# Sixteen on-chip copies of rounded q and k: issued from ScalarE's DMA queue instead of SyncE's

## The chip, the cores and the metric

The kernel runs on one core of one Trainium2 chip. The metric is device time in microseconds of one execution, as the median of several runs. The core has five engines that run side by side, each with its own in-order instruction queue: TensorE (PE, matrix products and transposes; its weight loads are shown apart as PEld), VectorE (DVE), ScalarE (ACT), GpSimd (POOL) and SyncE (SP, which computes nothing and here issues nearly all transfers). A transfer (DMA) is issued by an instruction on some engine's queue, and is then carried out by 16 DMA engines that belong to none of them. An instruction waits on semaphores until what it needs is done; while it waits, what stands behind it on its queue waits too.

## The reference, cut to what matters

Three blocks in a row, all in float32:

```python
# q, k, v: (2, 8, 768, 64); proj: (64, 6)
q_bits = einsum('bhsd,dk->bhsk', q, proj) > 0        # six sign bits for each row
k_bits = einsum('bhsd,dk->bhsk', k, proj) > 0
mask = bucket(q_bits)[..., :, None] == bucket(k_bits)[..., None, :]
scores = where(mask, q @ k.T / sqrt(64), -1e9)
attn = exp(scores - max(scores)); attn /= sum(attn) + 1e-9
x = (attn @ v) laid out as (2, 768, 512)

u = x + real(fft(fft(x, axis=1), axis=2))            # second block
un = layernorm(u)
y = u + relu(un @ w_ch1) @ w_ch2                     # 512 -> 2048 -> 512

theta = y @ w_theta                                  # third block
t = w_tok_r @ (y * cos(theta)) + w_tok_i @ (y * sin(theta))
out = (y + t) + relu((y + t) @ w_ch)
```

## The kernel before, in words

Precision is kept by splitting: an operand is stored as a rounded part and the remainder, and a product is taken as three (or fewer) products of the parts. Weights arrive as 64-bit floats and are turned into such pairs on the chip: a load into a tile `r` (`from_f64`, lines 169 to 181), two ScalarE activations and a VectorE operation on it, then a rounded copy by ScalarE (`w1h`, `w2h`) and a remainder by GpSimd (`w1l`, `w2l`). Every such load is issued on SyncE's queue, and reuses a tile that the GpSimd subtraction before has to be done with.

**The stages.** Attention of batch 0 runs first, two heads at a time (`attention_first`). Then come, interleaved, attention of batch 1 (`attention`, line 416), Fourier transform, layer norm and multilayer perceptron of batch 0, and the conversion of `w1` and `w2`. After that the same for batch 1, then the third block for both batches. In the trace attention of batch 1 prepares its first head at about 134 us and ends near 360 us; the multilayer perceptron of batch 0 begins inside it.

**Attention of batch 1.** `prep(b, j)` (lines 271 to 319) prepares a pair of heads: it loads q, k (tile `tt`) and v (`vr`), scales k, forms the sign bits with four matmuls per half, and then for each of the two heads fills a stack `s` (tag `stk`, two buffers) of four rows of [128, 768]: planes 0 and 1 are the left operand of the scores, planes 2 and 3 the right one. Since a head has only 64 dimensions, one half of the 128 partitions (`dd`) holds the rounded q or k, and the other half (`oo`) holds the remainder or a one-hot image of the bucket, which adds the mask to the scores in the same matmuls. Eight heads are prepared in this way, so each instruction of the loop over `h` (line 297) occurs eight times in the profile, once for q and once for k:

- ScalarE writes the rounded q (plane 0, line 302) and the rounded k (plane 2, line 305): `stk<-tt`.
- A DMA copies each of them to a second place in the same stack (lines 303 and 306): `stk<-stk`, on SyncE's queue. These are the lines of the change.
- GpSimd writes the remainders (lines 304 and 307): `stk<-tt,stk`.
- TensorE spreads the bits (`pat`), and ScalarE turns them into the one-hot halves (line 315): `stk<-pss,hb`.

`attn_S` (line 339) then takes four matmuls per block of 128 rows of q: `pss<-stk`. They need all planes. VectorE finds the maximum (`nm<-pss`), ScalarE takes the exponential (`p<-pss,nm`), ScalarE or GpSimd makes the rounded 16-bit part and GpSimd the remainder (`p<-p`, `pt<-p,pt`), a transposing DMA on SyncE's queue turns the block (`pt<-p`, `pt<-pt`, `x<-p`, by which buffer it uses), and TensorE multiplies with v (`pso<-vv,...`, `attn_AV`).

**What sets the order.** In this stage no order is written out by hand. Each piece of work gets a due time (`at(...)`, with a start, a pace per block, and a lead for `prep`), and a planner, which simulates the engines while the program is built, puts the instructions of each engine in one fixed order from the due times and from what it reckons to be ready. On the chip each queue keeps that order. The wrapper classes `AC`, `SY`, `PL`, `V`, `PE` (line 73) stand for the five queues.

Of the kernel before, what the change touches and what calls it, by code (L numbers as in the profile page):

```python
# [33 lines left out]
def f(t):  # L34
    return t.bitcast(F32)
# [35 lines left out]
def fused_kernel(ctx, tc, A, out):  # L71
    nc = tc.nc
    V, AC, PE, PL, SY = (Ordered(tc, e) for e in (nc.vector, nc.scalar, nc.tensor, nc.gpsimd, nc.sync))
# [4 lines left out]
    def mk(p, shape, dt, tag, **kw):  # L78
        return p.tile(shape, dt, tag=tag, name=tag, **kw)

    def mm(o, l, r, st, sp):
        PE.matmul(o, l, r, start=st, stop=sp)

    def pl_copy(out, in_, scale=1.0):
        PL.tensor_scalar(out=out, in0=in_, scalar1=scale, scalar2=0.0, op0=ALU.mult, op1=ALU.add)

    def stt(eng, out, in0, in1, op, scale=1.0):
        if eng is V:
            return V.scalar_tensor_tensor(out=out, in0=in0, scalar=scale, in1=in1, op0=ALU.mult, op1=op)
        assert scale == 1.0  # L90
        return eng.tensor_tensor(out=out, in0=in0, in1=in1, op=op)
# [23 lines left out]
    def PS(k):  # L115
        n = turn[k] % sum(c for _, c in ring[k])
        turn[k] += 1
        for p, c in ring[k]:
            if n < c:
                w = [128, 2, 512] if k == "s" else [128, 512]  # L120
                tag = "psm" if p in [x[0] for x in ring["m"]] else "ps" + k
                live[k] = p.tile(w, F32, tag=tag, name=tag)
                return live[k]
            n -= c
# [27 lines left out]
    def fill(n, k="o"):  # L152

        for _ in range(n):
            PE.matmul(live[k][:, 392:512], pat[:, 0], pat[:, 1, 0:120], start=True, stop=True)
# [115 lines left out]
    def prep(b, j):  # L271

        tt = mk(at_p, [128, 2, S], F32, "tt")
        ld = {"s": SY, "a": AC, "p": PL}[T["ld"][b]]
        vr = mk(at_p, [128, 2 * NT * (D + 1)], F32, "vr")
        for o, i in ((tt[:, 0], A["qT"]), (tt[:, 1], A["kT"]), (vr, A["v"])):
            ld.dma_start(out=o, in_=i[b, j])
        pl_copy(tt[:, 1], tt[:, 1], 0.125)
        v2 = mk(vv_p, [128, 2, 2 * NT * (D + 1)], F16, "vv")

        def values():
            AC.activation(out=v2[:, 0], in_=vr, func=AF.Copy, scale=VS)
            stt(V, v2[:, 1], vr, v2[:, 0], ALU.subtract, VS)

        if j:
            values()
        yield
        st = []
        bits = mk(at_p, [64, 2, 384], BF16, "bits")
        ps = PS("s")  # L290
        into = [ps[:, g, 0:384] for g in range(2)]
        for g in range(2):
            for qk in range(2):
                mm(into[g][32 * qk:32 * qk + 32], projb, tt[:, qk, 384 * g:384 * g + 384], True, True)
        V.tensor_scalar(out=bits, in0=ps[0:64, :, 0:384], scalar1=0.0, scalar2=None, op0=ALU.is_gt)
        made[4 * b + j] = [st, v2.rearrange("p a (h k c) -> p a h k c", h=2, k=NT)]
        for h in range(2):
            yield
            dd, oo = half[h], half[1 - h]
            s = mk(st_p, [128, 4, S], F32R, "stk")  # L300
            st.append(s)
            AC.activation(out=s[dd, 0], in_=tt[dd, 0], func=AF.Copy)
            SY.dma_start(out=f(s[dd, 1]), in_=f(s[dd, 0]))
            stt(PL, s[oo, 1], tt[dd, 0], f(s[dd, 0]), ALU.subtract)
            AC.activation(out=s[dd, 2], in_=tt[dd, 1], func=AF.Copy)
            SY.dma_start(out=f(s[oo, 3]), in_=f(s[dd, 2]))
            stt(PL, s[dd, 3], tt[dd, 1], f(s[dd, 2]), ALU.subtract)
            pp = PS("s")
            for g in range(2):
                mm(pp[:, g, 0:384], pat[0:64, h], bits[:, g], True, True)  # L310
            if b and not j and not h:
                fill(T["i0"])
            for qk in range(2):
                i = half[h if qk else 1 - h]
                AC.activation(out=s[oo, 2 * qk].rearrange("p (a n) -> p a n", a=2), in_=pp[i, :, 0:384],
                              func=AF.Sign if qk else AF.Relu, bias=hb[i, qk:qk + 1])
            if not j and not h:
                values()
        yield
# [96 lines left out]
    def attention(b, t0, pace, lead, hi_eng, lo_eng, after=lambda b, j: None):  # L416
        x_t[b] = mk(x_p, [128, NT, DM], F32, "x")
        n, w = 0, soft["p2"][0].shape[1]
        for j in range(4):
            i = 4 * b + j  # L420
            if i not in made:
                at(t0 + pace * n - lead)
                with after_gate("p1" if b else None):
                    run(prep(b, j))
            st, vv = made[i]
            for hh in range(2):
                h = PO[j] + 4 * hh
                at(t0 + pace * n)
                o = PS("o")[:, 0:NT * (D + 1)].rearrange("p (t d) -> p t d", t=NT)
                for t in range(NT):  # L430
                    at(t0 + pace * n)
                    ps = attn_S(st[hh], t)
                    fill(T["i1"][n] if n < len(T["i1"]) else 0)
                    with after_gate(0 if b and n >= T["n1"] else "ln0" if b and n >= T["n0"] else None):
                        p, m = attn_exp(ps)
                    if not t % w:
                        p2 = soft_tile("p2")
                    with after_gate(0 if b and n >= T["n1"] else None):
                        attn_split(p, p2[:, t % w].bitcast(F16).rearrange("p (a n) -> p a n", a=2), hi_eng(n), lo_eng(n))
                    if t % w == w - 1:  # L440
                        pt, trans = transposed(p2)
                        for i in range(w):
                            attn_AV(o, pt[:, 12 * i:12 * i + 12], vv, hh, t - w + 1 + i)
                    n += 1
                    if j < 3 and [hh, t] in T["ps"]:
                        at(t0 + pace * n - lead)
                        if [hh, t] == T["ps"][0]:
                            new = prep(b, j + 1)
                        next(new)
                at(t0 + pace * n - 30)  # L450
                attn_norm(b, h, o)
# [733 lines left out]
```

## Time and profile before

| | us |
|---|---|
| runs shown (3) | 729.13, 730.92, 737.44 |
| median | 730.92 |
| the profiled execution, whole | 728.28 |
| its span, first to last instruction | 726.5 |
| PE / PEld busy in the span | 664.8 / 510.9 |
| DVE / ACT / POOL busy in the span | 402.6 / 372.7 / 370.1 |

All times of rows are microseconds from the start of the profiled span, durations in a summary of a tile are nanoseconds. Line 62 is the helper through which almost every operation is issued, so the rows are told apart by their tiles: `stk<-tt` writes `stk` from `tt`. "SPq" is SyncE's queue. A row of the timeline gives the start, the time to the end of the last of its instructions, engine, line, operation, tiles, the count, and in brackets the idle time of the engine just before and what ended it. A row of a table of stretches gives the stretch, its length, then for PE, PEld, DVE, ACT and POOL the busy time with the number of instructions, then TensorE's granted clock (1.00 is its full speed), the share of the 16 DMA engines that was busy, and the rate of transfers. In a table of waits a row reads: who waited, for whom, total, number of times, longest.

### The profile page before, as it was taken

How to read it: one execution, taken by the hardware profiler on the slowest of the kernel's cores; microseconds unless marked ns; L12 is line 12 of the kernel's file. 1: busy time of each engine (PE TensorE's matmuls, PEld its weight loads, DVE VectorE, ACT ScalarE, POOL GpSimd, SP SyncE). 2: the span in 40 equal slices, each digit the busy share in tenths (PEclk: the TensorE clock that was granted, in tenths of full speed). 3: DMA queues.
4: the chain of work that ended last, by engine and by line, in shares of the span. 5: the costliest groups of instructions: out<-in, count | busy, mean ns of one | idle time of the engine just before them, and what ended most of it. 6: DMA issues, size and time to landing. Idle time of an engine off the chain costs nothing.

```text
span 726.5 us, 13450 instructions
## 1 busy us (share of the span) xinstructions
PE 664.8 (92%) x5424; PEld 510.9 (70%) x5424; DVE 402.6 (55%) x655; ACT 372.7 (51%) x597; POOL 370.1 (51%) x312
## 2 busy tenths in 40 slices
PE   5798988669668898999999999999999899999998
PEld 2365556557557655786686786687485599999997
DVE  1566787865999665543377583255422476751222
ACT  2565565766988898773423152065325676730010
POOL 3787789586878888776660020033403446930000
PEclk9999999978699999999999999999999999999999
DMA  9896967459889999776560043011004631720202
GB/s 327 186 187 141 157 121 142 93 164 213 197 206 240 269 231 253 151 145 124 102 195 27 13 120 65 1 45 30 1 1 145 223 89 39 234 81 25 88 1 87
DMA packets 161469, 93.68 MB, mean 129 GB/s; under 512 B 137088, under 2 KB 147584, under 8 KB 161408
## 3 DMA queue, kind: packets, MB, share of 16 engines
q1 hardware_dynamic: 159472, 86.27, 51.3%
q0 software_dynamic: 1936, 6.57, 2.6%
q8 instruction: 42, 0.69, 0.4%
q14 instruction: 19, 0.16, 0.1%
HBM read 49.82 MB, written 6.29 MB: 77 GB/s over the span
## 4 chain that ended last, share of the span: by engine, by line
PE 48%; POOL 10%; issue 9%; DMA 6%; ACT 5%; DVE 4%; POOLq 0%; SPq 0%; DVEq 0%; ACTq 0%
PE psm L62 31%; PE psf L62 14%; POOL p L62 3%; ACT r L62 2%; PE pso L62 2%; POOL w1l L62 2%; DMA x<-p 2%; POOL stk L62 2%; PE pss L62 1%; DMA r<-in_wtok 1%; DMA r<-in_w 1%; POOL pt L62 1%; DVE r L62 1%; ACT stk L62 1%; POOL w2l L62 1%
## 5 line engine op out<-in xcount | busy, mean ns | idle before, releaser
L62 PE MATMUL psm<-unT,w1h 128*128 128x256 f16 x768 | 130.4, 274 | 0.1
L62 PE MATMUL psm<-unT,w1l 128*128 128x256 f16 x384 | 105.2, 274 | 0.0
L62 DVE SCALAR_TENSOR_TENSOR r<-r 128x512 uint32<-128x512 uint32 (+1 forms) x64 | 64.6, 1016 | 51.9 <-ACT r L62 49.2
L62 PEld LDWEIGHTS <-w1h 128*128 128x128 f16 (+1 forms) x774 | 75.1, 99 | 15.5 <-issue 4.5
L62 PEld LDWEIGHTS <-hh 128*128 128x128 f16 x384 | 37.1, 98 | 42.8 <-issue 2.2
L62 POOL TENSOR_TENSOR w1l<-r,w1h 128x384 fp32r<-128x384 f32 (+1 forms) x36 | 41.9, 1178 | 43.5 <-ACT w1h L62 43.5
L62 PE MATMUL pss<-stk 128*128 128x384 f32 x192 | 48.8, 384 | 15.2 <-ACT p L62 9.4
L64 PE MATMUL pss<-stk 64*128 64x384 f32 (+1 forms) x288 | 55.4, 470 | 6.4 <-ACT p L64 3.2
L62 DVE TENSOR_REDUCE nm<-pss 128x1 f32<-128x768 f32 x48 | 44.9, 949 | 29.0 <-PE pss L62 28.8
L62 PE MATMUL psm<-w2h,hl 128*128 128x512 f16 x192 | 60.3, 379 | 0.0
L62 PE MATMUL psm<-w2l,hh 128*128 128x512 f16 x192 | 59.8, 379 | 0.2 <-POOL w2l L62 0.2
L62 ACT ACTIVATE r<-r,chalf 128x512 uint32<-128x512 uint32 (+1 forms) x64 | 46.1, 720 | 26.2 <-DMA r<-in_wtok 10.2
L62 PE MATMUL psm<-w2h,hh 128*128 128x512 f16 x192 | 59.3, 379 | 0.0
L62 POOL TENSOR_TENSOR p<-p,p 128x768 f16<-128x768 f32 x32 | 54.7, 1715 | 6.6 <-ACT p L62 5.5
L62 ACT ACTIVATE p<-pss,nm 128x768 f32<-128x768 f32 x48 | 42.5, 892 | 28.1 <-DVE nm L62 23.3
L62 DVE SCALAR_TENSOR_TENSOR hl<-psm,hh 128x512 f16<-128x512 f32 x48 | 32.8, 687 | 41.9 <-ACT hh L62 41.8
L64 DVE TENSOR_REDUCE nm<-pss 128x1 f32<-128x768 f32 x48 | 43.6, 950 | 19.9 <-PE pss L64 19.8
L62 ACT ACTIVATE hh<-psm 128x512 f16<-128x512 f32 x48 | 28.2, 590 | 40.4 <-PE psm L62 40.4
L62 PEld LDWEIGHTS pss<-stk 128*128 128x128 f32 x192 | 34.6, 204 | 20.2 <-ACT p L62 11.9
L62 PEld LDWEIGHTS <-w1l 128*128 128x128 f16 x384 | 37.7, 98 | 5.7 <-issue 1.2
L62 ACT ACTIVATE r<-r 128x512 f32<-128x512 f32 (+1 forms) x64 | 39.5, 618 | 0.0
L62 POOL TENSOR_TENSOR stk<-tt,stk 64x768 fp32r<-64x768 f32 x16 | 31.1, 1945 | 11.5 <-issue 9.6
(322 smaller groups left out, 1552.2 us busy)
## 6 DMA issues: line engine op xcount, KB each, us to landing
r<-in_w SPq DMA_DIRECT2D x32, 512.0 KB, 4.5
r<-in_wtok SPq DMA_DIRECT2D x24, 384.0 KB, 3.8
vr<-in_v SPq DMA_DIRECT2D x8, 390.0 KB, 3.6
stk<-stk SPq DMA_DIRECT2D x16, 192.0 KB, 3.8
xT<-xs SPq DMA_DIRECT2D x12, 256.0 KB, 2.6
xt<-xT SPq DMA_DIRECT2D x4, 768.0 KB, 5.8
ct<-in_ct POOLq DMA_DIRECT2D x4, 579.0 KB, 7.3
sn<-in_sn POOLq DMA_DIRECT2D x4, 576.0 KB, 8.2
```

Source lines behind the costliest of these rows:

```text
L62: return fn(*a, **k)
L64: self.last = fn(*a, **k)
```

## The change

Lines 303 and 306: the copies are issued with `AC.dma_start` instead of `SY.dma_start`. What is copied, from where to where, is the same, and nothing else is edited. The planner orders the program anew when it is built.

```diff
             AC.activation(out=s[dd, 0], in_=tt[dd, 0], func=AF.Copy)
-            SY.dma_start(out=f(s[dd, 1]), in_=f(s[dd, 0]))
+            AC.dma_start(out=f(s[dd, 1]), in_=f(s[dd, 0]))
             stt(PL, s[oo, 1], tt[dd, 0], f(s[dd, 0]), ALU.subtract)
             AC.activation(out=s[dd, 2], in_=tt[dd, 1], func=AF.Copy)
-            SY.dma_start(out=f(s[oo, 3]), in_=f(s[dd, 2]))
+            AC.dma_start(out=f(s[oo, 3]), in_=f(s[dd, 2]))
             stt(PL, s[dd, 3], tt[dd, 1], f(s[dd, 2]), ALU.subtract)
```

## Rows read from the trace of the kernel before

**Rows 1.** The page: span, and busy time of each engine in it.
```profile
span 726.5 us, 13450 instructions
PE 664.8 (92%) x5424; PEld 510.9 (70%) x5424; DVE 402.6 (55%) x655; ACT 372.7 (51%) x597; POOL 370.1 (51%) x312
```

**Rows 2.** Table of stretches: attention of batch 1, and what follows it.
```profile
133.00:325.00 192.00, 161.38 (x1592) 125.43 (x1591) 136.22 (x209) 154.98 (x231) 155.51 (x108) 0.91 0.89 200
325.00:525.00 200.00, 199.77 (x1476) 140.81 (x1474) 100.99 (x197) 73.53 (x125) 62.47 (x63) 1.00 0.29 68
525.00:726.00 201.00, 195.72 (x1155) 177.72 (x1153) 82.19 (x122) 76.08 (x144) 57.21 (x52) 1.00 0.29 92
```

**Rows 3.** Tile stk, from 133 to 325 us: counts, min/median/max duration, landing time.
```profile
L62 ACT ACTIVATE stk<-tt x16: 822/827/841, 133.8 to 316.0; 64x768 fp32r<-64x768 f32 x16
L62 SPq DMA_DIRECT2D stk<-stk x16: 461/472/953, 134.6 to 318.3; - x16
DMA to landing us min/median/max: 2.6/3.8/6.0
```

**Rows 4.** Waits of SyncE's queue, 133 to 325 us.
```profile
SPq L62 <- POOL w1l L62: 33.0, 15, 6.7
SPq L62 <- ACT stk L62: 15.0, 12, 6.7
```

**Rows 5.** Timeline of SyncE's queue: copies, and what stands by them.
```profile
134.62 2.80 SPq L62 DMA_DIRECT2D stk<-stk  x3
...
180.87 1.20 SPq L62 DMA_DIRECT2D stk<-stk  x2
185.88 2.85 SPq L62 DMA_DIRECT2D r<-in_w  x2
...
209.39 2.11 SPq L62 DMA_TRANSPOSE pt<-p  x1
211.55 0.61 SPq L62 DMA_DIRECT2D stk<-stk  x1
```

**Rows 6.** Timeline of ACT, POOL and PEld around the copies.
```profile
143.35 0.65 PEld L62 LDWEIGHTS pss<-stk 128*128 128x128 f32 x4 [1.65 <-ACT stk L62]
...
158.43 1.65 POOL L62 TENSOR_TENSOR p<-p,p 128x768 f16<-128x768 f32 x1
...
161.09 0.75 ACT L62 ACTIVATE r<-r,chalf 128x512 uint32<-128x512 uint32 x1 [3.36 <-DMA r<-in_w]
...
180.01 1.56 ACT L62 ACTIVATE stk<-tt 64x768 fp32r<-64x768 f32 x2
...
189.75 1.14 PEld L62 LDWEIGHTS pss<-stk 128*128 128x128 f32 x4 [3.67 <-ACT stk L62]
...
206.72 2.15 POOL L62 TENSOR_TENSOR p<-p,p 128x768 f16<-128x768 f32 x1
...
244.98 0.67 ACT L62 ACTIVATE w2h<-r 128x512 f16<-128x512 f32 x1 [2.61 <-DVE r L62]
```

**Rows 7.** Table of stretches: around the fifth to eighth copy and the last eight.
```profile
178.00:192.00 14.00, 7.20 (x55) 4.80 (x53) 13.62 (x27) 13.38 (x20) 10.07 (x7) 0.69 0.81 199
205.00:215.00 10.00, 7.16 (x83) 5.78 (x83) 9.78 (x36) 9.89 (x15) 9.69 (x7) 0.83 0.77 129
235.00:245.00 10.00, 9.58 (x106) 7.46 (x104) 7.56 (x7) 7.39 (x13) 8.12 (x6) 1.00 1.11 244
315.00:325.00 10.00, 10.00 (x124) 8.65 (x123) 4.56 (x6) 7.67 (x11) 8.76 (x6) 1.00 0.72 140
```

**Rows 8.** Waits of TensorE's weight loads for transposing DMAs, 133 to 325 us.
```profile
PEld L62 <- DMA pt<-pt: 5.4, 5, 1.8
PEld L62 <- DMA x<-p: 5.0, 4, 2.2
PEld L62 <- DMA pt<-p: 3.6, 3, 2.2
```

**Rows 9.** Table of stretches: five microseconds at a low granted clock.
```profile
185.00:190.00 5.00, 1.84 (x5) 1.33 (x6) 4.72 (x12) 4.70 (x7) 3.60 (x3) 0.50 0.49 125
```

## The prediction

> **What bounds the kernel now.** I read the page's busy times first, then tables of stretches, then the tile that the change touches, then the waits, and last the timeline around each copy.
>
> TensorE is busy 664.8 of 726.5 us [rows 1]. The stretches show where the rest is lost: from 325 us on it is busy 199.77 of 200 and 195.72 of 201, but from 133 to 325 us only 161.38 of 192 [rows 2]. So 30.6 us of idle TensorE lie in the very stretch in which attention of batch 1 is prepared and run, and all 16 copies lie there, from 134.6 to 318.3 us [rows 3]. Since TensorE's work is the same before and after, and the two later stretches leave it almost no gap, the change is worth what it adds to those 30.6 us or takes from them, together with what the clock does (0.91 on average there). In that stretch no single engine is the limit: ACT is busy 154.98 us and POOL 155.51 us of 192, near TensorE's own 161.38 [rows 2]. SyncE's queue mostly waits for others: 33.0 us for GpSimd's remainders of the weights, 15.0 us for the very activations that the copies need [rows 4]. The change moves work from a queue that mostly waits to an engine that is four fifths busy.
>
> **ScalarE takes over 16 issues.** No row shows ScalarE issuing a DMA, so the cost is bounded. Below: nothing, if the issue is worked off while another activation still runs in the engine. Above: on SyncE such an issue takes 0.472 us in the median and 0.953 at the longest [rows 3]. A copy must wait until its own activation has ended; two activations that follow each other without a copy take 1.56 us where each takes 0.827 [rows 6, 3], so 0.09 us of overlap is lost too. That makes 0.56 us for each copy by the median and 1.05 by the longest. I take 0.56, since in the code each copy stands right behind its activation; the nearest row, an issue of the same copy, is at 0.472. Sixteen of them are 9.0 us of ScalarE time, 0 to 16.8. Behind each copy stand, on ScalarE, the exponentials (for which TensorE's score tiles wait), the rounding of weights (for which GpSimd waits) and the one-hot activations (for which the score matmuls wait).
>
> What of it reaches the path differs from place to place:
>
> - Four copies from 134.62 on [rows 5]: 2.2 us. The first scores wait for ScalarE's one-hots at 143.35 [rows 6], so they come later by about this. But GpSimd takes up the first exponential's remainder only at 158.43, and ScalarE itself then stands idle for 3.36 us until 161.09, for a load [rows 6]. The cover is GpSimd's other work and this gap. Taken: 0; without the cover 2.2.
> - Two at 180.87 [rows 5]: ScalarE is busy 13.38 of the 14 us around them, and TensorE waits 3.67 us for a one-hot at 189.75 [rows 7, 6]. Nothing covers this: 1.1 us.
> - Two at about 209 and 211.55, one on either side of a transpose [rows 5]: ScalarE is busy 9.89 of 10 us, GpSimd 9.69, TensorE 7.16 [rows 7]. Taken in full: 1.1 us.
> - The last eight: around their first pair TensorE is busy 9.58 of 10 us, around the last 10.00 of 10 [rows 7]; it has the perceptron of batch 0 to do, and ScalarE has gaps such as 2.61 us at 244.98 [rows 6]. Taken: 0; without the cover 4.5.
>
> Together +2.2 us, with 0 and 9.0 as ends at the median price.
>
> **SyncE's queue loses 16 issues and their waits.** That is 16 x 0.472 = 7.6 us of issuing and up to 15.0 us of waiting [rows 3, 4]. It gains only where the next thing on the queue was ready. After the pair at 180.87 it is not: the next load goes out at 185.88, 3.8 us after the pair is done [rows 5], and GpSimd's remainder before it is what most of the queue's waits are for [rows 4]. At 209.39 a transpose whose input was done at 208.87 (206.72 + 2.15) goes out 0.5 us late behind a copy [rows 5, 6]. The other places of this kind lie where TensorE is full. Taken: -0.5; ends 0 and -7.6 (what the waits could add to that is the second rival). The second copy of that head, at 211.55, waits for the transpose in front of it and will go out about 2 us sooner; its stack still needs its GpSimd remainders and one-hots, so I cost this at nothing.
>
> **Landing of the copies.** They land 2.6 to 6.0 us after issue, 3.8 in the median [rows 3]. On a queue apart they may land up to 1.2 us sooner, or the loads and transposes that share the engines with them somewhat later. The waits on this tile that reach TensorE are for the activation (1.65 and 3.67 us in [rows 6]), and a copy issued by 182.07 has landed by 185.9, 3.8 us before the scores of 189.75 begin. Taken: 0, ends -1.2 and +1.2.
>
> The Trainium skill, in "DMA: Bandwidth & Descriptors", section "Issuing engines are not separate DMA queues", says that transfers issued by different engines run on the same 16 DMA engines and interleave, so that issuing from several saves only the sequencer's time to issue. By that rule no copy lands sooner for its own queue, and the gain of the change could not exceed the issuing time; the 15.0 us of waits on the queue speak against so tight a cap, since a queue held back by a wait delays what stands behind it too.
>
> **The planner.** It orders all engines anew. Nothing in the trace prices that; its ends are a share of the 30.6 us on either side. Taken: 0.
>
> **Sum.** 2.2 - 0.5 = +1.7 us on the profiled execution's 728.28 (726.5 of span and 1.8 around it): 730.0. The median of the three runs, 730.92, stands 2.6 above the profiled execution, so on the scale of the runs the sum is 732.6. I predict 732. The ends of the forecast's own terms: 728.28 - 3.8 = 724.5 (half of the issuing time gained, no cost), and 730.92 + 9.0 - 0.5, cut at 738, from where it is the first rival. So 724.5 to 738.
>
> **Rival 1: the copies hold up ScalarE.** If an issue on ScalarE is nearer to the longest row, the eight copies before 215 us, at 1.05 us each, push exponentials and one-hots back by 8.4 us, at a place where TensorE has nothing else to do. A later TensorE is also a slower one: from 185 to 190 us it is busy 1.84 of 5 us and its granted clock is 0.50, its 1.2 GHz level, with the engine idle while it waits for ScalarE [rows 9, 6]; five more microseconds of that kind at the busy share of such a stretch cost 0.9 us. 730.92 + 8.4 + 0.9 = 740. It decides from about 0.9 us on the path for each of eight copies (7.3 / 8). For it: ScalarE at 13.38 of 14 and 9.89 of 10 [rows 7]. Against it: the cover named for the first four, and a planner that can put another activation ahead of a copy so that the wait is over when the copy's turn comes. Chance 0.26.
>
> **Rival 2: SyncE's queue, freed, brings transposes and loads forward.** TensorE's weight loads wait 14.0 us for the three kinds of transposes (5.4 + 5.0 + 3.6) [rows 8], all on that queue. If the 22.6 us that the copies hold it (7.6 + 15.0) were what delays them, or if the new order does the same by luck, ten of these 14.0 go: 730.92 - 10 = 721. For it: a copy waiting for an activation does block transposes, as at 209.39. Against it: at 185.88 and most other places the queue waits for GpSimd next, and GpSimd is no faster [rows 4, 5]. By the skill's rule above the gain would end at the issuing time; with the row's 0.472 us that is 728.28 - 7.6 = 721 too, so the rule lowers the chance of more and not the time. Chance 0.22.
>
> **Rival 3: nothing moves.** The planner puts the copies where ScalarE waits anyway, or the issue is hidden beneath a running activation, and SyncE's queue only waits longer for GpSimd: 728 to 731. For it: the gaps of 3.36 and 2.61 us; against it, 13.38 of 14. Chance 0.07.
>
> **How the numbers follow.** The forecast itself has the remaining 0.45. A measurement of this kernel can tell about 1% (7.3 us) from no change. Forecast and rival 3 lie within it, 0.52; rival 1 is slower, 0.26; rival 2 faster, 0.22. The range leaves out the outer parts of both rivals, about 0.1 on either side: 720 to 743, where the forecast's own is 724.5 to 738.
>
> **What would show it.** Right: `stk<-stk` on ScalarE's queue, 16 of them; ScalarE's busy time hardly changed but gaps of half a microsecond behind `stk<-tt`; the wait of SyncE's queue for `ACT stk` gone and that for GpSimd's remainders longer; TensorE's busy time from 133 to 325 us within 5 us of 161. Rival 1 would show in longer waits of TensorE for `ACT stk` and `ACT p`, and a lower clock between 143 and 215 us; rival 2 in the 14.0 us of waits for transposes at half or less. I am wrong if an issue on ScalarE holds it for well over a microsecond, or if the order of the stage is so different that the stretches can no longer be laid side by side.

## The result, and the profile after

The changed kernel takes 740.72 us in the median of four runs (737.01 to 743.45), the kernel before 731.38 in four runs beside it. The ratio is 1.0137, with a 95% interval of 1.0095 to 1.0178: 1.4% slower; the two medians lie 9.3 us apart. That lies in the predicted range (720 to 743), but 8.7 us above the predicted time, outside the range of the likeliest case (724.5 to 738), and on a side that had been given 0.26.

The profiled execution took 743.45 us, the longest of the four. The page of the changed kernel, span and busy times [rows 1]:

```profile
span 741.7 us, 13461 instructions
PE 678.6 (91%) x5424; PEld 519.5 (70%) x5424; DVE 405.2 (55%) x655; ACT 374.5 (50%) x597; POOL 370.6 (50%) x312
```

ScalarE is busy 374.5 us where it was 372.7. This alone says little, since the page does not count an instruction that issues a DMA as busy; what the issues cost is read from the timeline below. TensorE does the same 5424 matmuls in 678.6 us instead of 664.8. The table of stretches of the changed kernel (columns as in [rows 2]) shows where the time goes, with the first stretch of the kernel before ahead of it:

```profile
0.00:40.00 40.00, 27.71 (x154) 13.02 (x154) 13.93 (x24) 15.99 (x21) 21.10 (x27) 1.00 0.88 254
...
0.00:40.00 40.00, 29.15 (x139) 13.02 (x140) 13.65 (x22) 14.10 (x19) 18.64 (x24) 0.70 0.83 252
...
133.00:325.00 192.00, 157.88 (x1488) 122.25 (x1487) 135.51 (x211) 151.33 (x226) 148.32 (x105) 0.88 0.87 195
```

What the first 40 us show is no work of the change. The order of the instructions is the same in both kernels up to about 133 us, yet the granted clock is 0.70 there, against 1.00 in the kernel before. The changed kernel's profile enters the stage 3.3 us late (the first `stk<-tt` at 137.08 instead of 133.77), and of its 15.2 us over the profile of before 11.9 are left for the stage itself. From 133 to 325 us, 1488 matmuls get done instead of 1592 (the late start included), at a clock of 0.88 instead of 0.91.

Tile `stk` in the changed kernel, activations, copies, and the time in which the copies land [rows 3]:

```profile
L62 ACT ACTIVATE stk<-tt x16: 823/826/842, 137.1 to 324.4; 64x768 fp32r<-64x768 f32 x16
L62 ACTq DMA_DIRECT2D stk<-stk x16: 468/486/992, 141.1 to 325.2; - x16
DMA to landing us min/median/max: 4.1/4.7/9.8
```

An issue takes on ScalarE's queue what it took on SyncE's (486 ns and 472 in the median). But the copies land after 4.7 us instead of 3.8, and after 9.8 at the longest, where it was 6.0. The waits of TensorE's weight loads for transposing DMAs in the changed kernel [rows 8]:

```profile
PEld L62 <- DMA pt<-p: 8.4, 6, 2.3
...
PEld L62 <- DMA pt<-pt: 7.3, 4, 3.5
...
PEld L62 <- DMA x<-p: 4.2, 3, 2.4
```

Together 19.9 us, where they were 14.0. The waits of SyncE's queue [rows 4] show the other side: that for `ACT stk` (15.0 us) is gone.

```profile
SPq L62 <- POOL w1l L62: 30.6, 14, 6.1
SPq L62 <- POOL w2l L62: 29.5, 15, 3.9
```

The queue got nothing for it. All its waits in this stretch come to 129.8 us where they were 125.4, those for GpSimd to 101.3 where they were 96.9. The wait for `w2l` rose most, from 13.6 to 29.5, but this is mostly the planner's order: in the runs of the next section, with the old order and the copies on ScalarE it is 13.8, with the new order and the copies on SyncE 24.5.

Last the timeline of ScalarE around the first four copies [rows 5 and 6 show them before]:

```profile
139.41 1.57 ACT L62 ACTIVATE stk<-tt 64x768 fp32r<-64x768 f32 x2
141.01 0.77 ACT L62 ACTIVATE r<-r,chalf 128x512 uint32<-128x512 uint32 x1
141.08 1.14 ACTq L62 DMA_DIRECT2D stk<-stk  x2
141.68 0.67 ACT L62 ACTIVATE r<-r 128x512 f32<-128x512 f32 x1
142.25 0.77 ACT L62 ACTIVATE r<-r,chalf 128x512 uint32<-128x512 uint32 x1
142.26 1.64 ACTq L62 DMA_DIRECT2D stk<-stk  x2
```

No ACT row has idle time in brackets: the activations follow each other without a gap while the queue issues four copies (ACTq). The planner put the copies behind another activation than their own, where nothing is left to wait for, and an issue is worked off beside a running activation. At none of the 16 does ScalarE stand idle behind `stk<-tt` for more than 0.03 us.

### The profile page after: what moved, and what is told of

It reads as the page before. It is cut to its first block, busy times and chain, and to the rows that moved or that the text cites. A ratio compares the mean times of both kernels' runs of the same rounds, so it can differ in the third digit from the quotient of the medians.

```text
span 741.7 us, 13461 instructions
## 1 busy us (share of the span) xinstructions
PE 678.6 (91%) x5424; PEld 519.5 (70%) x5424; DVE 405.2 (55%) x655; ACT 374.5 (50%) x597; POOL 370.6 (50%) x312
## 4 chain that ended last, share of the span: by engine, by line
PE 47%; DVE 8%; DMA 8%; issue 8%; ACT 5%; POOL 5%; ACTq 0%; SPq 0%; POOLq 0%; DVEq 0%
PE psm L62 30%; PE psf L62 13%; DMA pt<-p 3%; ACT r L62 2%; DMA r<-in_w 2%; DVE r L62 2%; DMA r<-in_wtok 1%; PE pso L62 1%; PE pss L62 1%; DVE fa L62 1%; POOL w2l L62 1%; ACT stk L62 1%; POOL w1l L62 1%; DVE u L62 1%; ACT p L62 1%
## 5 line engine op out<-in xcount | busy, mean ns | idle before, releaser
L64 PE MATMUL pss<-stk 64*128 64x384 f32 (+1 forms) x288 | 60.2, 506 | 5.6 <-ACT p L64 3.0
```

Of the source, the lines that this page charges most:

```text
L64: self.last = fn(*a, **k)
```

## The experiments

All ratios are to the kernel before, run on the same chip in the same set. Where it is said that the order is kept, the order of every engine was written down from the built program and laid upon the planner:

```diff
+def keep_order(tc):
+    traced = {i.name: i for i in tc.nc.cur_bb.bb.instructions}
+    for v in kept_order().values():
+        v = [x for x in v if x in traced]
+        for a, b in zip(v, v[1:]):
+            tc.add_manual_dep(traced[b], a, mybir.DependencyInfo(
+                mybir.DependencyClass.NoSync, mybir.DependencyReason.DATA), reason="kept order")
```

The letters of theories hold within the set of runs in which they are quoted.

### Queue and order taken apart

**The queue alone.** Order of the kernel before; each copy on ScalarE one activation behind its own.

```diff
-            SY.dma_start(out=f(s[dd, 1]), in_=f(s[dd, 0]))
+            AC.dma_start(out=f(s[dd, 1]), in_=f(s[dd, 0]))
...
-            SY.dma_start(out=f(s[oo, 3]), in_=f(s[dd, 2]))
+            AC.dma_start(out=f(s[oo, 3]), in_=f(s[dd, 2]))
...
+    keep_order(tc)
```

> The copies go out from ScalarE's queue, but the order of all other instructions on all five engines is that of the kernel before, imposed by edges; each copy stands behind one activation more than its own. Theory A (the time came from the new order that the planner dealt, and issuing on ScalarE costs its computing next to nothing): the time of before within 0.4%, ratio 0.996 to 1.004. Theory B (rival 1: ScalarE is held by its issues): 16 issues of 0.49 us, about eight of them on the path, so 4 to 8 us more, ratio 1.006 to 1.012.

Measured: 742.38 us, ratio 1.0156 (1.0111 to 1.0201). The move of the queue alone, in the old order, costs as much as the whole change. Theory A is wrong, and the loss is also above the range of theory B.

**The same, with the copy right behind its own activation.** The edit is the same; only the place of the copies in the order kept differs.

> As the kernel with the kept order, but each copy stands directly behind its own activation on ScalarE's queue, so that the queue waits there for the activation to end. Theory A: the wait is now exposed, some 0.5 us of gap behind each of the 16 activations, 8 us of ScalarE's time, of which the eight before 215 us reach the path in part: ratio 1.000 to 1.007, and gaps of 0.4 to 0.7 us on ScalarE behind each copy. Theory B: no different from the kernel with one activation between, since the issue costs the same wherever it stands.

Measured: 737.92 us, ratio 1.0107 (1.0072 to 1.0142), not slower than with the copy one activation later, and above the range of theory A. The timeline of ScalarE in this kernel has the gap that I had put into the sum:

```profile
133.61 0.83 ACT L62 ACTIVATE stk<-tt 64x768 fp32r<-64x768 f32 x1
134.47 0.50 ACTq L62 DMA_DIRECT2D stk<-stk  x1
135.02 0.84 ACT L62 ACTIVATE stk<-tt 64x768 fp32r<-64x768 f32 x1 [0.58 <-ACT stk L62]
```

Behind the 16 copies the gaps are 0.55 to 0.60 us, where I had worked out 0.56. So the price was right for a copy in this place. What the gaps cost the kernel this pair of runs does not settle: with them the second copy of a head also goes out 1.39 us behind the first instead of 0.73, and the transposing DMAs beside the copies, which the next section is about, land at other times too (at the last head after 6.6 us instead of 9.1).

**The order alone.** Order of the changed kernel, copies on SyncE's queue.

```diff
+    keep_order(tc)
```

> The copies are issued by SyncE as in the kernel before, but the order of all other instructions is the one that the planner dealt for the changed kernel, imposed by edges. Theory A: as slow as the changed kernel, ratio 1.009 to 1.018 to the kernel before. Theory B: most of the loss is gone, ratio 0.998 to 1.005.

Measured: 734.72 us, ratio 1.0093 (1.0061 to 1.0125). The new order costs something by itself; theory A holds, at the low end of its range. Its copies land within 5.3 us. The two parts do not add up: 1.56% for the queue in the old order, 0.93% for the order, 1.37% for both. In the new order the queue thus adds 0.44 points, less than the two intervals can tell from nothing.

**k's copies alone, in an order that the planner made for them.**

```diff
-            SY.dma_start(out=f(s[oo, 3]), in_=f(s[dd, 2]))
+            AC.dma_start(out=f(s[oo, 3]), in_=f(s[dd, 2]))
```

> Only the copies of k go out from ScalarE's queue, those of q stay on SyncE's; the planner orders it anew, and its order is neither that of before nor that of the changed kernel. Theory A: a third deal, with a time of its own that half the issues do not foretell, anywhere from 0.99 to 1.02. Theory B: half of the change, half of its loss, ratio 1.005 to 1.009.

Measured: 738.89 us, ratio 1.0138 (1.0100 to 1.0177). Half of the copies cost as much as all of them, more than theory B allowed. A third order is mixed in here, so this run alone decides nothing; with the old order the same edit comes further down.

### Where the time goes

With the order kept, the trace can be laid beside that of before, instruction by instruction. The run enters the stage 1.2 us early, and up to 210 us ScalarE never loses that lead altogether. Then it falls behind in steps, and the steps lie where TensorE waits for a transposing DMA of SyncE's queue that flew beside the copies of a head. At heads 3, 4, 5 and 7 (the first is 0) one such wait grew from 1.90 to 2.83 us, from 0.42 to 1.61, from 1.70 to 3.37 and from nothing to 3.09; the largest step is at the last head (copies at 320 us). Timeline of that place before:

```profile
316.10 0.46 SPq L62 DMA_DIRECT2D stk<-stk  x1
...
316.66 1.50 SPq L62 DMA_TRANSPOSE pt<-p  x1
...
318.25 0.95 SPq L62 DMA_DIRECT2D stk<-stk  x1
```

DMA issues of the kernel before from 316 to 318.5 us (columns: KB each, median time to landing in us):

```profile
stk<-stk SPq DMA_DIRECT2D x2, 192.0 KB, 3.0
pt<-p SPq DMA_TRANSPOSE x1, 3.9
```

And with the order kept and the copies on ScalarE's queue, the timeline, first the issues, then who waited:

```profile
319.83 0.49 ACTq L62 DMA_DIRECT2D stk<-stk  x1
319.84 2.21 SPq L62 DMA_TRANSPOSE pt<-p  x1
...
320.56 0.47 ACTq L62 DMA_DIRECT2D stk<-stk  x1
...
328.97 1.17 PE L62 MATMUL pso<-vv,pt 128*128 128x65 f16 x18 [3.09 <-DMA pt<-p]
```

with its DMA issues from 319.5 to 321 us:

```profile
stk<-stk ACTq DMA_DIRECT2D x2, 192.0 KB, 5.6
pt<-p SPq DMA_TRANSPOSE x1, 9.1
```

The same three transfers are issued within 0.73 us instead of 2.15, and the transpose lands after 9.1 us instead of 3.9. TensorE waits 3.09 us for it. The table of stretches, first the kernel before, then the run with the order kept:

```profile
318.00:328.00 10.00, 10.00 (x100) 7.56 (x98) 3.90 (x5) 6.91 (x10) 7.30 (x6) 1.00 0.74 142
...
322.00:332.00 10.00, 6.91 (x64) 5.44 (x61) 2.63 (x4) 4.64 (x7) 5.68 (x4) 0.83 0.97 141
```

TensorE is busy 6.91 of 10 us where it was busy 10.00, and the granted clock is 0.83 over these 10 us instead of 1.00: from 329 to 332 us, right behind the wait, it is 0.50, the 1.2 GHz level. So this place costs more than the wait itself: TensorE is 3.7 us late before it and 8.4 us after it. Over the stage the clock is 0.89 in this run, 0.91 before. This made the theory for the next runs: two queues in which a copy and a transpose are in flight slow each other, while one queue sends them one behind the other.

**Only the heads without such a transpose** (0, 1, 2 and 6; 3, 4, 5 and 7 stay), order kept. At heads 2 and 6 of the run above a transpose had been issued some 3 us ahead of the copies and was landing.

```diff
-            SY.dma_start(out=f(s[dd, 1]), in_=f(s[dd, 0]))
+            (AC if 2 * j + h in (0, 1, 2, 6) else SY).dma_start(out=f(s[dd, 1]), in_=f(s[dd, 0]))
...
-            SY.dma_start(out=f(s[oo, 3]), in_=f(s[dd, 2]))
+            (AC if 2 * j + h in (0, 1, 2, 6) else SY).dma_start(out=f(s[oo, 3]), in_=f(s[dd, 2]))
```

> Order of all engines as in the kernel before; only the eight copies of heads 0, 1, 2 and 6 are issued by ScalarE, the copies of heads 3, 4, 5 and 7 stay on SyncE's queue. Theory C (two queues: a copy and a transposing DMA in flight side by side slow each other; these four heads had no transpose beside their copies in the run with the order kept): no loss, ratio 0.996 to 1.004, and landing of the longest copy under 6.5 us. Theory A (the issue itself costs ScalarE its time, every copy the same): half of the loss of the run with the order kept, ratio 1.008 (1.005 to 1.011). Theory B (what is lost is only chance of the new state of the clock): anything up to 1.016.

**Only the heads with one**, order kept; the edit is the same with `(3, 4, 5, 7)`.

> The other half: order as in the kernel before, only the copies of heads 3, 4, 5 and 7 are issued by ScalarE. Theory C: nearly all of the loss of the run with the order kept, ratio 1.010 to 1.018; transposes that fly beside a copy land after 8 us or more at the longest, where it was 6.1 before. Theory A (every copy costs the same): half of it, ratio 1.008 (1.005 to 1.011).

Measured: 729.43 us, ratio 1.0007 (0.9979 to 1.0036), for the heads without; 738.43 us, ratio 1.0126 (1.0087 to 1.0165), for those with. Theory C holds for both. Eight issues on ScalarE cost nothing in one place and nearly the whole loss in another, so it is not the issue. Nor is it the gaps: in either run four of the eight copies leave ScalarE idle for 0.55 to 0.63 us. Landing of all 16 copies, first in the kernel with heads 0, 1, 2 and 6 moved:

```profile
DMA to landing us min/median/max: 2.5/3.4/6.1
```

and with heads 3, 4, 5 and 7 moved:

```profile
DMA to landing us min/median/max: 2.6/4.6/10.0
```

With these heads moved, the transposes issued within a microsecond of the copies land after 8.6 to 10.6 us; in the kernel before, the same ones took 3.9 to 7.4 (not 6.1 at the most, as I had written).

**The same in the changed kernel itself.** It and the run with the new order and the copies on SyncE's queue have the same order on every engine, so their traces can be laid side by side as well. At head 3 the transpose next to the copies, and TensorE's wait for it, first with the copies on SyncE's queue, then in the changed kernel:

```profile
pt<-pt SPq DMA_TRANSPOSE x1, 5.5
213.93 0.73 PE L62 MATMUL pso<-vv,pt 128*128 128x65 f16 x18 [0.35 <-DMA pt<-pt]
...
pt<-pt SPq DMA_TRANSPOSE x1, 9.9
224.61 0.73 PE L62 MATMUL pso<-vv,pt 128*128 128x65 f16 x18 [3.25 <-DMA pt<-pt]
```

At head 4 a transpose lands after 10.6 us; at heads 5, 6 and 7 none next to the copies takes over 7.4. So the disturbance is in the changed kernel too, but as strong at two heads only instead of four.

**q's copies alone, and k's alone**, in the order of before: one of the two edits of the first experiment each.

> Order of all engines as in the kernel before; only the copies of q, one for each head, are issued by ScalarE, the copies of k stay on SyncE's queue. By the measurements apart, one copy on a second queue beside a transpose costs nothing to speak of (4.8 us against 4.5), a pair costs 3 us. Theory P (it takes a pair on the second queue): ratio 0.997 to 1.005, no transpose beside a copy lands later than 7.5 us. Theory C1 (any copy on a second queue beside a transpose, if SyncE's queue holds more than the transpose): about half of the loss of the run with the order kept, 1.005 to 1.011.

> The same with the copies of k alone on ScalarE's queue, order as in the kernel before. Theory P: ratio 0.997 to 1.005; what the earlier run with k alone lost (1.0138) then came from its own order. Theory C1: 1.005 to 1.011. If only the copy of k matters (it is the one into the other half, and the later of the two): 1.010 to 1.018, and that of q alone 1.000.

Measured: 729.59 us, ratio 0.9975 (0.9952 to 0.9999), for q; 734.82 us, ratio 1.0055 (1.0033 to 1.0076), for k. These two expectations rest on the measurements of the next part. q alone costs nothing; k alone costs a third of what both cost. No theory holds for both: P foretold q and not k, C1 foretold k and not q, and the third case (k's copy alone matters) gave k too much. Together the two halves make +0.3%, both at once +1.6%: most of the loss needs both copies of a head on the second queue. In the run with q alone no transpose lands later than 7.7 us; with k alone three land after 8.1, 8.6 and 9.8, at heads 3, 4 and 5.

### The transfers by themselves

Four kernels hold nothing but the transfers, in eight phases of six repetitions each: the transpose is the kernel's (128x1536 of 16 bits), the copies are of its size (64x768 of 32 bits). The core of the first:

```diff
+                if what == "t":
+                    eng.dma_start_transpose(out=pt, in_=big[:, 1].bitcast(F16))
+                elif what == "c":
+                    eng.dma_start(out=cp[0:64, 0], in_=big[0:64, 0])
+                elif what == "d":
+                    eng.dma_start(out=cp[64:128, 1], in_=big[0:64, 0])
...
+            "c": [("c", SY), ("t", SY), ("d", SY)],
+            "d": [("c", AC), ("t", SY), ("d", AC)],
```

> Measures the disputed cost by itself; of the reference nothing is computed, zeros are written. Eight phases, six times each, nothing else running: (a) the kernel's transposing DMA (128x1536 of 16 bits) alone on SyncE's queue; (b) two copies of 64x768 alone on ScalarE's queue; (c) copy, transpose, copy all on SyncE's queue; (d) the same three, copies on ScalarE's queue, transpose on SyncE's; (e) a load of 128x1024 from DRAM alone; (f) copy, load, copy on SyncE's queue; (g) copies on ScalarE's queue beside the load; (h) one copy on either queue. Theory C: the last of (c) lands at most 7 us after the first issue; in (d) transpose and second copy land after 8 to 10 us, though two queues could start them sooner; (g) is no longer than (f) by over 1 us if it is the transpose that suffers, as long as (d) is against (c) if any two queues disturb each other. Rival (the two queues share the engines without loss, and what was seen in the kernel comes from its other traffic): (d) is no longer than (c), both under 7 us.

The view of the transfers of this kernel, phase (c) (78 to 124.8 us), then phase (d) (124.8 to 190.9 us): for 40 slices of the phase the busy share of the DMA engines in tenths and the GB/s that they moved, then the issues, with KB each and the median time to landing in us:

```profile
DMA  0059960008993003899000599500089910058970
GB/s 0 0 118 177 243 134 0 0 0 173 205 221 74 0 0 71 165 223 211 3 0 0 131 185 233 123 0 0 16 179 214 224 39 0 0 110 169 239 154 0
...
cp<-big SPq DMA_DIRECT2D x12, 192.0 KB, 3.0
pt<-big SPq DMA_TRANSPOSE x6, 4.0
...
DMA  0499810079930029992005998100799500099920
GB/s 0 89 168 94 104 21 0 0 133 182 101 60 0 0 61 175 101 111 27 0 0 99 168 86 107 16 0 0 121 185 85 79 6 0 17 172 139 108 41 0
...
cp<-big ACTq DMA_DIRECT2D x12, 192.0 KB, 5.5
pt<-big SPq DMA_TRANSPOSE x6, 8.7
```

From first issue to last landing, the three take 5.5 us in the median on one queue (from 79.72 to 85.32 the first time), and 8.7 on two (from 137.19 to 145.70). Alone, the transpose takes 3.7 and the pair of copies 3.4. One after the other without any overlap they would take 7.1, so the two queues are slower than no overlap at all. In phase (d) the transpose and the second copy both land at the end; the first copy lands after 3.0 us. Copies and a load from DRAM in place of the transpose take 6.2 us on one queue and 4.8 on two. But that load goes out 1.07 us behind the first copy, not at the same instant as the transpose does, so these runs do not show that a load at that moment would go unharmed.

**Which partner.** The phases differ in what flies beside the transpose.

```diff
+            "a": [("t", SY), ("c", AC)],
+            "b": [("c", SY), ("t", SY)],
...
+            "g": [("c", PL), ("t", SY), ("d", PL)],
+            "h": [("c", AC), ("t", AC), ("d", AC)],
```

> What must the partner be for a transposing DMA to slow down? Of the reference nothing is computed, zeros are written. Eight phases, six times each: (a) transpose on SyncE's queue beside one copy of 64x768 on ScalarE's; (b) the same two, both on SyncE's; (c) a load of 128x1024 from DRAM on ScalarE's queue beside the transpose; (d) both on SyncE's; (e) two transposes, one on either queue; (f) both on SyncE's; (g) two copies on GpSimd's queue beside the transpose; (h) copy, transpose, copy all on ScalarE's queue. Theory C1 (any second queue disturbs a transpose): against their one-queue partners (a), (c) and (g) take longer from first issue to last landing, (g) about the 8.7 us that the pair on ScalarE's queue took, and (h) the 5.6 us of one queue. Theory C2 (it is the copy between partitions of the core itself, or ScalarE's queue, that disturbs): (c) is no longer than (d), and (g) near 5.6 us if it is ScalarE's queue. Two transposes (e) against (f): C1 says longer; if they share fairly because their packets are alike, the same.

Measured, first issue to last landing: one copy on the second queue 4.9 us (a), on the same 4.5 (b); a load on the second queue, 1.6 us behind the transpose, 5.3 to 5.5 (c, the three repetitions with that distance), on the same 5.6 to 5.8 (d); the pair on GpSimd's queue 7.3 (g); all three on ScalarE's queue 5.5 (h). So ScalarE's queue is not to blame: all on it is as quick as all on SyncE's, and GpSimd's queue hurts too. But not any second queue hurts: C1 fails on (c), and on (a) the difference is 0.4 us. Phases (e) and (f) tell nothing, since the second transpose in (e) was issued only when the first had landed.

**Which property of the pair.**

```diff
+            "a": [("d", AC), ("t", SY)],
+            "b": [("c", AC), ("t", SY), ("e", AC)],
...
+            "f": [("g", AC), ("t", SY)],
```

> Alone, one copy beside a transpose cost little (4.8 us for both), two copies much (8.7 us; the second went into the other half of the partitions and landed late). Which is it? Of the reference nothing is computed, zeros are written. Eight phases, six times each; transpose on SyncE's queue, copies on ScalarE's unless said: (a) one copy into the other half; (b) two copies, both within their half; (c) two copies, both into the other half; (d) one copy within its half, issued about 1 us later than the transpose, behind an activation; (e) the same into the other half; (f) one copy of twice the size, over all 128 partitions; (g) the same two on SyncE's queue; (h) the pair as in the kernel (one within, one into the other half). Theory X (the copy into the other half disturbs): (a) and (e) at 7 us or more for both to land, (b) and (d) under 6, (c) longest. Theory Y (a copy that is in flight while the transpose writes; the first copy only escapes by being early): (b), (c) and (h) all near 8.7, (d) and (e) alike at 6 or more, (f) longer than (g) by 1 us or more.

DMA issues of this kernel: one copy into the other half (a), two copies within their half (b), one copy of twice the size (f):

```profile
pt<-big SPq DMA_TRANSPOSE x6, 4.9
...
pt<-big SPq DMA_TRANSPOSE x6, 8.8
...
cp<-big ACTq DMA_DIRECT2D x6, 384.0 KB, 3.1
pt<-big SPq DMA_TRANSPOSE x6, 4.9
```

Neither where the copies go nor the bytes of a single copy matter; a second copy on the second queue does. Both theories of this set fall: X on (b), Y on (f) and on the single copy issued later (5.0 us).

**The pair split over the queues, or later, or smaller.**

```diff
+            "a": [("c", SY), ("t", SY), ("d", AC)],
+            "b": [("c", AC), ("t", SY), ("d", SY)],
...
+            "d": [("w", AC), ("C", AC), ("D", AC), ("t", SY)],
+            "e": [("1", AC), ("t", SY), ("2", AC)],
```

> q's copies alone on the second queue cost the kernel nothing, k's half a per cent, both 1.6. In the kernel the pair's other copy stands on SyncE's queue ahead of the transpose (k alone) or behind it (q alone). Measured apart, of the reference nothing is computed, zeros are written; eight phases, six times each: (a) copy and transpose on SyncE's queue, second copy on ScalarE's (k alone); (b) first copy on ScalarE's, transpose and second copy on SyncE's (q alone); (c) all three on SyncE's; (d) the pair on ScalarE's about 1 us after the transpose; (e) the pair on ScalarE's, each copy of half the size; (f) one copy on ScalarE's, one on GpSimd's queue, beside the transpose; (g) the pair on ScalarE's; (h) as (a), the second copy about 1 us later. Theory P (a transpose with two copies in flight beside it, of which the later is on another queue): (a), (f), (g) 7 us or more from first issue to last landing, (b) and (c) under 6.3. If it takes two copies on one other queue: (a), (b), (c), (f) under 6.3 and only (d), (g) near 8.7. If bytes decide: (e) near the 4.8 us of one whole copy; if the number of transfers: (e) near 8.

DMA issues of this kernel, the transposes of the phases (a), (b), (d), (e), (f) and (g) in this order:

```profile
pt<-big SPq DMA_TRANSPOSE x6, 5.0
...
pt<-big SPq DMA_TRANSPOSE x6, 4.9
...
pt<-big SPq DMA_TRANSPOSE x6, 4.9
...
pt<-big SPq DMA_TRANSPOSE x6, 5.6
...
pt<-big SPq DMA_TRANSPOSE x6, 5.7
...
pt<-big SPq DMA_TRANSPOSE x6, 8.7
```

Only (g) is slow, the pair as the run with the order kept issues it at the last head: one copy at the same instant as the transpose, the second half a microsecond later, both on one other queue. Split over two queues (a, b, f) it is not, nor if the pair comes 0.9 and 1.4 us behind the transpose (d), nor with copies of half the size (e), though (e) and (f) lose a little. In (a) the copy on the other queue went out half a microsecond ahead of the transpose; in (h), 0.35 us behind it, the transpose takes 5.1. My expectation that it takes two copies on any queues is wrong; that it takes two on one other queue holds, but without other traffic only with this timing.

## Why the prediction was right or wrong

**The bound: right.** The time is lost in the stretch from 133 to 325 us. TensorE waits there, its clock falls from 0.91 to 0.88, and the engines' own work has not grown.

**ScalarE takes over 16 issues: +2.2 taken, about 0 measured.** An issue is 0.486 us, near the 0.472 I took for it, and the gap behind a copy right after its activation is 0.55 to 0.60 against 0.56. But the planner left no such gap, and the runs with eight issues moved (1.0007 and 0.9975) price them at nothing. The lower bound, an issue worked off beneath a running activation, was the right end.

**SyncE's queue loses its waits: -0.5 taken, no gain seen.** As argued, waits for GpSimd take the place of the copies' (in all 96.9 to 101.3 us; with the old order and the copies on ScalarE 106.5).

**Landing of the copies: 0 taken, with ends of 1.2 us. This is the step that failed, together with the planner's below.** I had looked at how soon a copy lands and whether anything waits for the copy. That transposes might land "somewhat later" I had written in half a sentence, with 1.2 us as the end and no row for it; and of the copy at 211.55 I had seen that it would go out 2 us sooner, that is beside the transpose, and priced this at nothing. The copies' median rose by 0.9 us, but with the order kept a transpose went from 3.9 to 9.1 us; TensorE waits for it, and its clock falls behind the wait. In the old order the term belonged at some +9 to +11 us: 1.26 and 1.56% of 730 by the two runs with the order kept in which these heads' pairs are moved. In the changed kernel's own order it is smaller, about +3 us by the 0.44 points, and not clear of the noise.

The Trainium skill's rule that I had weighed ("DMA: Bandwidth & Descriptors", section "Issuing engines are not separate DMA queues") says that transfers from several issuers interleave on the same DMA engines, and that only issuing time is saved. The trace agrees as far as it goes: on their own queue the copies land after 4.1, 4.7 and 9.8 us (shortest, median, longest), where it was 2.6, 3.8 and 6.0. That section does not say that the interleaving can cost: 8.7 us against 5.5 for the same three transfers. There the measurement decides.

**The planner: 0 taken, +0.9% measured** for its order with the copies on SyncE (0.6 to 1.25%). That is about 7 us, the larger part of the loss if the order is changed first and the queue second. I could not price it, and said so; a share of the 30.6 us of idle time on either side did hold it. Which instruction of that order costs the time I have not traced. That the queue adds less in the new order fits the two heads with a slow transpose instead of four; that this is the whole reason is argued, not shown.

**Rival 1: right in time, wrong in cause.** It gave 740, and 740.72 was measured. But ScalarE is not held up: it has no gap behind the 16 activations, and where four copies do leave gaps the kernel takes as long as before (1.0007). Of the signs named for this rival the lower clock came, 0.74 instead of 0.79 from 143 to 215 us, but not the longer waits: those of the weight loads for `ACT p` fell from 11.9 to 7.5 us, and those for `ACT stk` stayed at 6.5. That the time fits says nothing for the mechanism. **Rival 2** is out: waits for transposes went up (14.0 to 19.9 us), not down. **Rival 3** holds for its reason (issues hidden beneath activations, SyncE's queue waiting longer for GpSimd) and fails for what it left out.

**The signs named beforehand.** The 16 copies on ScalarE's queue, its unchanged busy time, the vanished wait for `ACT stk`, and TensorE's 157.88 us, within 5 of 161, all came true, and none of them could tell the forecast from what happened; the busy time could not have failed, since issues are not counted in it. The gaps behind `stk<-tt` did not come. The landing times, which I had not put on the list, were the sign. One slip in the range: its own lower end, 724.5, is reckoned from the profiled execution and its upper end from the median of the runs; from the median the lower end is 727.1.

**What stays open.** Why a pair with this timing is so slow. The condition found apart does not cover the kernel: there k's copies alone still cost 0.55%, with transposes landing as late as 9.8 us, and in the changed kernel the transpose of 10.6 us had gone out 1.6 us ahead of its pair. Loads fly there at the same time; whether they stand in for the second copy no run shows. And the runs with the order kept spread from 736.28 to 744.41 with nothing in the program that differs.

## What to carry to other kernels

Before a transfer is given a queue of its own, list the transposing DMAs that are issued within a microsecond or two of it, and price the change at what these would lose, not only at what the transfer's issue costs. Where a planner orders the program anew, run the new order with the old queue as well: here it cost 0.93% by itself. A queue on which much waits may be what keeps a transpose and its neighbours one behind the other. In the profile after, read the landing times of the neighbours, not only of the transfer that was moved.

## What the runs showed of the hardware that I had not expected

- Three transfers of 192, 384 and 192 KB (copy, transpose, copy) take 5.5 us from one queue, either of two, and 8.7 us when the pair is on another queue than the transpose and starts with it. In the second case the DMA engines are shown as busy but move less: in phase (d) of the measurement apart, slices with a busy share of 8 or 9 tenths move 85 to 185 GB/s, in phase (c) 165 to 243. With the pair on GpSimd's queue the three take 7.3 us.
- A DMA issue on ScalarE's queue (0.47 to 0.49 us in the median) runs beside the activations, unless the copy has to wait for the activation just ahead of it; then the next activation starts 0.55 to 0.63 us late.
- A wait of 3.09 us for one late transpose cost TensorE 4.7 us at that place, with the granted clock at 0.50 from 329 to 332 us, behind the wait, where the kernel before had 1.00.
- Moving half of a pair can cost nothing where moving the whole costs 1.6%. The prices of two moved transfers must not be added.
